# A fused forward and backward kernel: w_down in four buffers, the first projection activations on POOL's queue, and the last accumulations interleaved with held matmuls

## The chip, the cores and the metric

The kernel runs on one core of one Trainium2 chip. The metric is the device time of one execution in microseconds (us). A core has TensorE (PE: matmuls, with weight loads on a queue of their own, PEld), VectorE (DVE), ScalarE (ACT), GpSimd (POOL) and SyncE (SP). SP and POOL issue the DMA transfers here; all transfers share the core's 16 DMA engines.

## The reference

The kernel computes the output of one adaLN block and the gradients of all its inputs for a given grad_out. S = 2048 tokens, D = 576, F = 4608, all bf16.

```python
mod = (silu(c) @ w_mod).reshape(1, 6, 1, D)      # sa, ca, ga, sb, cb, gb
h = layernorm(x) * (1 + ca) + sa
x = x + ga * irfft2(rfft2(h) * (w_r + 1j * w_i)) # over tokens and channels
h = layernorm(x) * (1 + cb) + sb
g, u = h @ w_gate, h @ w_up                      # D -> F, twice
x = x + gb * ((g * u) @ w_down)                  # F -> D
out, vjp = jax.vjp(f, A_x, A_w_r, A_w_i, B_w_gate, B_w_up, B_w_down, c, w_mod)
return out, *vjp(grad_out)
```

out_0 is the output, out_1 the gradient of x, out_2 and out_3 those of the two filters, out_4, out_5 and out_6 those of w_gate, w_up and w_down, out_7 and out_8 those of c and w_mod.

## The kernel before

The tokens lie in 16 tiles t of 128 rows, F in 36 blocks fb of 128. The program is written for one core, and a scheduler turns it into one instruction order per engine. It goes by priorities and data dependences. Three things overrule it: `tc.issue_after(x)` (and the helper `behind`) places an instruction behind another one in its queue's order; `pe_order(seq)` chains a given list of TensorE instructions; and a pool's buffer can be loaded again only when its last reader is done.

The kernel starts with the forward Fourier part and the first half of the backward pass. The main loop over fb follows. For each block it computes the gate and up products (gup), their elementwise products hh, gg and gu, a store of hh to DRAM (`hhT_d`, on POOL's queue), DMA transposes of the three into `hh_sf`, `gg_sf` and `gu_sf` (SP's queue, pool `sfp`), the weight gradients (`product(fb, i)`, tile u57p, TensorE line L613, evacuated by ScalarE at L615), and the gradient of h (`u8_output`, tile u8p, L694), which VectorE adds into the accumulator `acc(t)` at L699. `product(fb, 0)` multiplies hh_sf with `gon` (grad_out times gb, 2304 KB resident) and its result goes to out_6 at L634; the other two multiply gg_sf and gu_sf with `h2p` and go to out_4 and out_5, by a DMA transpose into woT.

Past the loop, the last two blocks are left over. Their u8p sums run for every t: 32 outputs of four matmuls, 128 in all. Their six weight-gradient products, 2 x 3 x 32 = 192 matmuls, are collected in `held` and serve as filler. The transposes of the last block (fb = 35) have a lowered priority (`-2 * HEAD_START`).

Stage 1 then runs the backward of the second layernorm and the column and row transforms of its result, one tile t per step k, in four pipelined steps. `t1_norm` loads n2c, goc and yc (L902, SP's queue, five buffers each), copies acc to `ghr` (L916), and computes the gradient `gxr`, which POOL's queue stores to gx1_d (L920; the rings of ghr and gxr have three rows). At t = 1 and 2 it also loads the tables RD and G (`T_RD`, `T_G`) on SP's queue. `t1_turn` transposes gxr on TensorE (trp) and sums columns (colsum L830, diag L837), `t1_cols` multiplies with RD (zp, L944) and `t1_rows` with G1 (vp, L951 and L952). Stage 2 is the transform over tokens and its filter, stage 3 the way back and the backward of the first layernorm, whose results ob go to out_1 on SP's queue.

The output projection (u3p, L1168) is the last part: for each t, two halves of 36 matmuls with `hl` (hh read back from hhT_d, 576 KB for nine blocks and two tiles, `hl_load`) as weights and w_down as the moving operand. ScalarE copies the result to ob3 (L1169); VectorE multiplies it and adds, and POOL's queue stores it. w_down is resident: `wdA` holds its first 15 blocks, `wdB` the other 21. `wn` holds the filters' transformed weights for the filter gradients. The matmuls of t = 0 to 5 (`proj`) are filler too: `deal` goes through the TensorE instructions of stages 1 to 3, tile step by tile step, and puts a fixed number of fillers behind each, held ones first.

Loads of the projection's data (L982, all on SP's queue) are chained one behind another by `queued`: three parts of wdA behind the yc loads of tiles 7, 9 and 11, the first part of wdB behind that of tile 12, four hl, two parts of wn, two parts of wdB. In SBUF, wdA lies where wT was, wdB where wT's end, the transposed operands (hh_sf, gg_sf, gu_sf) and part of gon's neighbours were, and the first hl where gon was; a buffer pool is released as a whole, when the last instruction that reads from it has run.

During the projection, 14 filter gradients (`filter_grad`, `more_grads`) run on VectorE, two per tile from t = 5, each after a load Xn. Five `section` calls compute gradients of w_mod in the tiles of `late`: they evacuate two PSUM halves (one on ScalarE, one on VectorE), load wmj and store o8. A sixth, for MGB, comes at the end.

Of the kernel before, what the change touches and what calls it, by code (L numbers as in the profile page):

```python
# [19 lines left out]
NT = 16  # L20
S = 2048
D = 576
# [62 lines left out]
def build(ctx, tc, A_x, A_w_r, A_w_i, B_w_gate, B_w_up, B_w_down, c_in, w_mod, grad_out,  # L85
# [48 lines left out]
    def traced():  # L134
        return len(nc.cur_bb.bb.instructions)
# [3 lines left out]

    def pe_order(seq):  # L140

        for a, b in zip(seq, seq[1:]):
            tc.add_manual_dep(b, a.name, mybir.DependencyInfo(mybir.DependencyClass.NoSync, mybir.DependencyReason.DATA), reason="order of PE")

# [414 lines left out]
    with ExitStack() as ms:  # L559
# [14 lines left out]
        with ExitStack() as bs:  # L574
# [6 lines left out]
            wtp = bpool("wtp", 2)  # L581
            sfp = bpool("sfp", 2)
            sop = bpool("sop", 1)
# [91 lines left out]
            def turn_items(fb):  # L675
                def turns_():
                    hhT, ggT, guT = trip[fb][2:5]
                    nc.gpsimd.dma_start(hhT_d[:, :, fb, :].rearrange("tp f x -> f tp x"), hhT[:].rearrange("f (tp ti) p -> f tp (ti p)", ti=2))  # L678
                    sfs[fb] = []
                    for nm, srcT in (("hh_sf", hhT), ("gg_sf", ggT), ("gu_sf", guT)):  # L680
                        sf = sfp.tile([128, NT, 128], BF, name=nm)
                        with tc.high_priority(-2 * HEAD_START if fb == NFB - 1 else 0):
                            turned = nc.sync.dma_start_transpose(out=sf[:], in_=srcT[:].rearrange("f t p -> f (t p)"))
# [23 lines left out]
            for fb in range(NFB):  # L707
                if fb % FBW == 0:
                    wgu = wp.tile([128, 9, FBW * 128], BF, name="wgu")
                    for wi_, wsrc in enumerate((B_w_gate, B_w_up)):  # L710
                        eng = nc.sync if wi_ == 0 else nc.gpsimd
                        with later(wi_, fb):
                            eng.dma_start(wgu[:, 4 * wi_:4 * wi_ + 4, :], wsrc[0:512, fb * 128:(fb + FBW) * 128].rearrange("(m q) f -> q m f", q=128))
                            eng.dma_start(wgu[64 * wi_:64 * wi_ + 64, 8, :], wsrc[512:576, fb * 128:(fb + FBW) * 128])
                if fb == 0:
                    wTs[0] = wT_load(0, turns[-1:] * 5)
                ghh = ghp.tile([128, NT, 128], BF, name="ghh")
                with later(1, fb):
# [31 lines left out]
    with ExitStack() as ts:  # L750
# [16 lines left out]
        oAp = pool("oAp", 1)  # L767
        oBp = pool("oBp", 1)
        tl = pool("tl", 1)
# [37 lines left out]
        def deal(held, proj):  # L807
            more, seq = held + proj, []
            for n, (stage, k, ins) in enumerate(staged):
# [9 lines left out]
            pe_order(seq)  # L819

# [65 lines left out]
        with ExitStack() as r1:  # L886
# [11 lines left out]
            def t1_norm(t):  # L898
                for k, src in (("n2c", n2_d), ("goc", go_v), ("yc", y_d)):
                    ld[k, t] = c1.tile([128, D], BF, name=k, bufs=5)  # L900
                    with behind(ld["order"]):
                        ins = nc.sync.dma_start(ld[k, t][:], src[:, t, :])  # L902
                ld["final"] = ld["y", t] = ins.ins
                if t in (1, 2):
# [14 lines left out]
                norm_back(c1, gn, n2, rstd2g[:, t:t + 1], ld["goc", t][:], gx, "2")  # L919
                nc.gpsimd.dma_start(gx1_d[:, t, :], gx)  # L920

# [53 lines left out]
        wn = ra.tile([128, 2, NT, FP], BF, name="wn2")  # L975
        wdA = oAp.tile([128, 15, D], BF, name="wdA")
        wdB = oBp.tile([128, NFB - 15, D], BF, name="wdB")
        last = [None]

        def queued(behind_, dst, src):  # L980
            with behind([i_ for i_ in (behind_, last[0]) if i_ is not None]):
                last[0] = nc.sync.dma_start(dst, src).ins  # L982

        def wd_load(f0, n, behind_=None):
            dst = wdA[:, f0:f0 + n, :] if f0 < 15 else wdB[:, f0 - 15:f0 - 15 + n, :]
            queued(behind_, dst, B_w_down[f0 * 128:(f0 + n) * 128, :].rearrange("(j f) d -> f j d", f=128))

        def hl_load(nq, behind_=None):
# [5 lines left out]
            queued(behind_, hl[:], hhT_d[nq // 4, :, 9 * (nq % 4):9 * (nq % 4) + 9, :])  # L994
            return hl

        slot = [-1]
# [157 lines left out]
        for tp_ in range(NT // 2):  # L1155
# [5 lines left out]
            for ti in range(2):  # L1161
# [3 lines left out]
                for h in range(2):  # L1165
                    p2 = ps_u3.tile([128, 512], FP32, name="u3p")
                    for fb in range(NFB):
                        mm = nc.tensor.matmul(p2[:, 0:288], lhsT=hls[fb // 9][:, fb % 9, ti * 128:(ti + 1) * 128], rhs=(wdA[:, fb] if fb < 15 else wdB[:, fb - 15])[:, h * 288:(h + 1) * 288], start=(fb == 0), stop=(fb == NFB - 1))  # L1168
                    nc.scalar.copy(ob[:, h * 288:(h + 1) * 288], p2[:, 0:288])  # L1169
                if t in late:  # L1170
                    with tc.issue_after(mm.ins):
                        section(*late[t], secp)
                pr = prs[t] = o2p.tile([128, D], BF, name="pr3", bufs=3)
# [5 lines left out]
                nc.vector.tensor_tensor(out=o0[:], in0=of[:], in1=x1t[:, ti, :], op=ADD)  # L1179
                stored = nc.gpsimd.dma_start(o0_v[:, t, :], o0[:])  # L1180
                more_grads(t)
                if 11 <= t < 15:
# [87 lines left out]
```

## Time and profile before

| what | value |
|---|---|
| time, median of 3 runs (lowest, highest) | 1599.67 us (1598.83, 1602.9) |
| the profiled execution's own time | 1602.26 us |
| its span | 1600.5 us |
| granted TensorE clock, mean | 0.982 |
| busy: TensorE / VectorE / ScalarE / GpSimd | 95% / 65% / 35% / 11% |
| busy us of TensorE, VectorE | 1520.9, 1036.0 |
| DMA | 280.19 MB, mean 175 GB/s |

Times of single events below are microseconds from the start of the span of this one execution. "Busy" is the time in which an engine executed instructions. A row of the timeline has start, duration, engine, line, operation, output and input tiles, and in brackets the idle time ahead of it with what ended it. Matmuls are pipelined, so the listed durations of neighbours overlap: about 0.285 us is the duration of one with 288 columns, while a long row of them shows how far apart they start. The clock column of a stretch is the clock that the throttle granted, as a share of full speed: 1.00 is all of it, and where it is lower, some of the matmuls there ran at a lower rate.

The parts of the span are: up to about 1243 us the transforms, the main loop and the first half of the backward pass; 1243 to 1269 the lead (the last u8p sums); 1269 to 1331 stage 1; up to 1380 the change to stage 2; stages 2 and 3 up to 1475; then the projection of the remaining tiles, and from 1580 the end (the MGB section and out_7).

| stretch (us) | TensorE busy | VectorE busy | clock | DMA share |
|---|---|---|---|---|
| 1240 to 1270 | 25.89 of 30 | 25.06 | 1.00 | 0.90 |
| 1270 to 1330 | 59.30 of 60 | 42.97 | 1.00 | 0.70 |
| 1330 to 1380 | 25.24 of 50 | 10.96 | 0.73 | 0.74 |
| 1470 to 1490 | 12.39 of 20 | 13.77 | 0.83 | 0.80 |
| 1520 to 1530 | 5.58 of 10 | 9.06 | 0.86 | 0.52 |

### The profile page before, as it was taken

The numbers are of one execution on the slowest core, as the hardware profiler recorded it, in microseconds if no ns is written. First come the engines' busy times: TensorE is split into PE (matmuls) and PEld (weight loads), VectorE is DVE, ScalarE is ACT, GpSimd is POOL, SyncE is SP. The second block draws the span as 40 slices with busy tenths as digits, with TensorE's granted clock in tenths as the row PEclk, the third lists the DMA queues.
The fourth block names the chain that finished last, engine by engine and source line by source line (L and its number), as shares of the span: only waits on it lengthen the run. The fifth ranks groups of instructions, "written<-read, shape, count | busy, mean of one in ns | idle before, by whom it ended". The sixth has DMA issues, their size and how long they took to land.

```text
span 1600.5 us, 30060 instructions
## 1 busy us (share of the span) xinstructions
PE 1520.9 (95%) x11300; PEld 1031.5 (64%) x11306; DVE 1036.0 (65%) x2627; ACT 554.6 (35%) x1136; POOL 180.6 (11%) x289
## 2 busy tenths in 40 slices
PE   6999889999999999999999999999999895898987
PEld 4666533566676666666666666667666673687765
DVE  7866743666666666666666666666665871668674
ACT  6667722322222222222222222222222362566031
POOL 0001212100010101001010101001000311100124
PEclk9999999999999999999999999999999998899998
DMA  9869997869685785877777776957865877544775
GB/s 320 271 193 246 279 226 215 161 135 167 123 166 126 158 157 110 167 133 154 144 150 131 141 162 130 171 109 159 149 136 107 239 191 238 184 139 140 299 240 141
DMA packets 491652, 280.19 MB, mean 175 GB/s; under 512 B 408913, under 2 KB 463826, under 8 KB 490482
## 3 DMA queue, kind: packets, MB, share of 16 engines
q1 hardware_dynamic: 466466, 187.75, 54.7%
q0 software_dynamic: 25040, 90.53, 19.2%
q8 instruction: 88, 1.44, 0.4%
q14 instruction: 58, 0.48, 0.1%
HBM read 108.33 MB, written 82.31 MB: 119 GB/s over the span
## 4 chain that ended last, share of the span: by engine, by line
PE 79%; DMA 6%; issue 6%; DVE 5%; ACT 2%; POOL 1%; SPq 1%; POOLq 0%; ACTq 0%; DVEq 0%
PE u57p L613 26%; PE u8p L694 17%; PE gup L665 15%; PE u4p L424 6%; PE u3p L1168 6%; PE gup L660 2%; DMA Xn<-xn_d 2%; DMA wdB<-in_B_w_down_dram 1%; PE zp L944 1%; PE zp L362 1%; ACT u L798 1%; DMA ghhT_d<-ghh_st 1%; DMA hh_sf<-hhT 1%; DVE goT L395 1%; PE u4p L419 1%
## 5 line engine op out<-in xcount | busy, mean ns | idle before, releaser
L699 DVE TENSOR_TENSOR acc<-acc,u8p 128x288 f32<-128x288 f32 x1088 | 489.1, 453 | 314.9 <-PE u8p L694 314.5
L694 PE MATMUL u8p<-wT,ggT 128*128 128x288 bf16 x1152 | 327.7, 286 | 3.5 <-DVE acc L699 3.2
L694 PE MATMUL u8p<-wT,guT 128*128 128x288 bf16 x1152 | 327.4, 286 | 0.0
L665 PE MATMUL gup<-h2T,wgu 128*128 128x512 bf16 x1152 | 294.9, 379 | 0.0
L615 ACT CAST so<-u57p 128x288 bf16<-128x288 f32 x216 | 86.0, 398 | 512.4 <-PE u57p L613 504.0
L613 PE MATMUL u57p<-h2p,gg_sf 128*128 128x288 bf16 x1152 | 189.4, 286 | 0.0
L613 PE MATMUL u57p<-gon,hh_sf 128*128 128x288 bf16 x1152 | 187.9, 286 | 0.3 <-DMA hh_sf<-hhT 0.3
L613 PE MATMUL u57p<-h2p,gu_sf 128*128 128x288 bf16 x1152 | 187.5, 286 | 0.0
L665 PEld LDWEIGHTS <-wgu 128*128 128x128 bf16 x1152 | 109.5, 98 | 98.8 <-issue 17.1
L694 PEld LDWEIGHTS <-ggT 128*128 128x128 bf16 x1152 | 112.6, 98 | 67.2 <-issue 14.0
L424 PE MATMUL u4p<-goT,wdT 128*128 128x512 bf16 x656 | 152.5, 382 | 0.6 <-DVE goT L396 0.5
L1168 PEld LDWEIGHTS <-hl 128*128 128x128 bf16 x1152 | 110.5, 100 | 65.2 <-DMA hl<-hhT_d 19.9
L694 PEld LDWEIGHTS <-guT 128*128 128x128 bf16 x1152 | 112.7, 98 | 58.2 <-issue 5.0
L613 PEld LDWEIGHTS <-hh_sf 128*128 128x128 bf16 x1152 | 112.4, 98 | 28.9 <-DMA hh_sf<-hhT 0.6
L613 PEld LDWEIGHTS <-gu_sf 128*128 128x128 bf16 x1152 | 112.4, 98 | 28.6
L613 PEld LDWEIGHTS <-gg_sf 128*128 128x128 bf16 x1152 | 112.3, 98 | 28.1
L667 ACT CAST gT<-gup 128x512 bf16<-128x512 f32 x144 | 84.3, 585 | 130.7 <-PE gup L665 130.7
L1168 PE MATMUL u3p<-wdB,hl 128*128 128x288 bf16 x672 | 101.3, 290 | 15.6 <-DMA wdB<-in_B_w_down_dram 14.0
L667 ACT CAST uT<-gup 128x512 bf16<-128x512 f32 x144 | 84.3, 585 | 73.6 <-PE gup L665 73.6
L424 PEld LDWEIGHTS <-wdT 128*128 128x128 bf16 x656 | 61.6, 98 | 74.4 <-issue 9.9
L1168 PE MATMUL u3p<-wdA,hl 128*128 128x288 bf16 x480 | 77.8, 301 | 21.1 <-DMA hl<-hhT_d 16.6
L678 POOL DMA_DIRECT2D hhT_d<-hhT x36 | 33.2, 921 | 481.9 <-DVE hhT L669 452.9
(358 smaller groups left out, 1671.9 us busy)
## 6 DMA issues: line engine op xcount, KB each, us to landing
ghhT_d<-ghh_st POOLq DMA_DIRECT2D x36, 512.0 KB, 4.5
ghh<-ghhT_d POOLq DMA_DIRECT2D x36, 512.0 KB, 7.5
hhT_d<-hhT POOLq DMA_DIRECT2D x36, 512.0 KB, 6.5
hl<-hhT_d SPq DMA_DIRECT2D x32, 576.0 KB, 7.8
out_dram<-woT SPq DMA_DIRECT2D x72, 128.0 KB, 2.0
wdn<-in_B_w_down_dram SPq DMA_DIRECT2D x18, 288.0 KB, 3.7
out_dram<-so SPq DMA_DIRECT2D x36, 144.0 KB, 2.9
wgu<-in_B_w_gate_dram SPq DMA_DIRECT2D x18, 256.0 KB, 3.3
```

What stands on the lines that cost most here:

```text
L362: mm = nc.tensor.matmul(zp[:, :FP], lhsT=hTs[t][:, m, :], rhs=T["RD"][:, m, cc, :], start=(m == 0), stop=(m == 4))
L395: nc.vector.tensor_tensor(out=goT[:, t, :, :], in0=pt[:, 0:5, :], in1=gbT[:].unsqueeze(2).to_broadcast([128, 5, 128]), op=MUL)
L424: nc.tensor.matmul(pt[:], lhsT=wdTs[k][:, j, m, :], rhs=goT[:, 4 * sb4:4 * sb4 + 4, m, :], start=(m == 0 and n == 5), stop=(m == n - 1))
L613: mm = nc.tensor.matmul(pw[0][:, 0:288], lhsT=sf[:, t, :], rhs=rhs_n[:, t, h * 288:(h + 1) * 288], start=(t == 0), stop=(t == NT - 1))
L615: nc.scalar.copy(so[:, h * 288:(h + 1) * 288], pw[0][:, 0:288])
L660: nc.tensor.matmul(pts[-1][:], lhsT=wgu[r, 8, jw * 128:(jw + 1) * 128], rhs=h2T[r, 4 * sb4:4 * sb4 + 4, 4, :], start=True, stop=False)
L665: nc.tensor.matmul(pts[k][:], lhsT=wgu[:, 4 * wi_ + m, jw * 128:(jw + 1) * 128], rhs=h2T[:, ts_, m, :], start=False, stop=(m == 3))
L667: nc.scalar.copy((gT, uT)[wi_][:, ts_, :], pts[k][:])
L678: nc.gpsimd.dma_start(hhT_d[:, :, fb, :].rearrange("tp f x -> f tp x"), hhT[:].rearrange("f (tp ti) p -> f tp (ti p)", ti=2))
L694: nc.tensor.matmul(pu[:, 0:288], lhsT=l_, rhs=r_, start=(k == 0), stop=(k == len(mms) - 1))
L699: nc.vector.tensor_tensor(out=dst, in0=dst, in1=pu[:, 0:288], op=ADD)
L1168: mm = nc.tensor.matmul(p2[:, 0:288], lhsT=hls[fb // 9][:, fb % 9, ti * 128:(ti + 1) * 128], rhs=(wdA[:, fb] if fb < 15 else wdB[:, fb - 1 ...
```

## The change

The change has six parts.

- w_down lies in four buffers: wdA as before and `wdB0`, `wdB1`, `wdB2` with seven blocks each, every one in a pool of its own. The transposed operands get a pool for each kind (`sfh`, `sfg`, `sfu`), and gon gets the pool `res5`. The SBUF addresses are the same; each new buffer now overlies fewer old ones.
- The loads of wdA, wdB0, wdB1, the first four hl, wn and the last part (wdB2) move from SP's to POOL's queue. Each has a place between two gx1 stores: behind the store of tile 3 the first, and so on to tile 15. wdB2 has no fixed place and is queued behind wn. Later hl loads stay on SP's queue.
- The hl loads numbered 12 to 17 use the six-slot ring instead of the pool `hlp`, which takes its first seven from number 18 on.
- The last u8p sums are put into an order of their own on TensorE: eight of them (one t), then three held matmuls, sixteen times (`lead`). The other 144 held matmuls are dealt 8 per tile step of stage 1, where before it was 24, 16, 12 and then 10 per step, from 192.
- The filter gradients of the projection come 3, 4, 4 and 3 at t = 5, 7, 9 and 11. The sections come at t = 6, 8, 10, 12 and 13, are written behind the output's own operations, and evacuate both halves on ScalarE (the last section, MGB, as before).
- `pe_order` is renamed `in_order` and also chains POOL's loads and stores.

```diff
-            sfp = bpool("sfp", 2)
+            sfp = [bpool("sf" + k, 2) for k in "hgu"]
...
-    gonf = res2.tile([128, NT * D + 64], BF, name="gon")
+    res5cm = tc.tile_pool(name="res5", bufs=1, reuse_waits="tile")
+    res5 = res5cm.__enter__()
+    gonf = res5.tile([128, NT * D + 64], BF, name="gon")
...
+            mark = traced()
             for t in range(NT):
                 for h in range(2):
                     u8_output([NFB - 2, NFB - 1], t, h)
+            sums = pe_since(mark)
             mark = traced()
             for i in range(3):
                 for fb_ in (NFB - 2, NFB - 1):
                     for f in product(fb_, i):
                         f()
             held = pe_since(mark)
+            lead = []
+            for t in range(NT):
+                lead += sums[8 * t:8 * t + 8] + held[3 * t:3 * t + 3]
+            held = held[3 * NT:]
+        res5cm.__exit__(None, None, None)
...
         def deal(held, proj):
-            more, seq = held + proj, []
+            more, seq = held + proj, list(lead)
...
                 if stage == 1:
-                    q = 24 if k == 0 else 16 if k == 1 else 12 if k == 2 else 10
+                    q = 8
...
-                evac(dmb[:, h * 288:(h + 1) * 288], halves[h](), eng=("a" if h == 0 else "v"))
+                evac(dmb[:, h * 288:(h + 1) * 288], halves[h](), eng=("v" if last and h else "a"))
...
-                nc.gpsimd.dma_start(gx1_d[:, t, :], gx)
+                ld["gx", t] = nc.gpsimd.dma_start(gx1_d[:, t, :], gx).ins
...
+        wds = [(0, oAp.tile([128, 15, D], BF, name="wdA"))] + [(15 + 7 * k, oBp[k].tile([128, 7, D], BF, name="wdB%d" % k)) for k in range(3)]
...
-            if nq >= 12 and (nq - 12) % 13 < 7:
+            if nq >= 18 and (nq - 18) % 13 < 7:
                 hl = hlp.tile([128, 9, 256], BF, name="hl2")
...
-        for k in range(0, 15, 5):
-            wd_load(k, 5, ld["y", 7 + 2 * (k // 5)])
-        wd_load(15, 7, ld["y", 12])
-        first_hl = [hl_load(nq, ld["y", 13 + nq // 2]) for nq in range(4)]
+        def queued_load(t, f, *args):
+            hl = f(*args, ld["gx", t])
+            if t < NT - 1:
+                in_order([last[nc.gpsimd], ld["gx", t + 1]])
+            return hl
+
+        for k in range(3):
+            queued_load(3 + 2 * k, wd_load, 5 * k, 5)
+        queued_load(8, wd_load, 15, 7)
+        first_hl = [queued_load(9 + nq, hl_load, nq, nc.gpsimd) for nq in range(3)]
+        queued_load(12, wd_load, 22, 7)
+        first_hl.append(queued_load(13, hl_load, 3, nc.gpsimd))
         for c in range(2):
-            queued(ld["final"], wn[:, c].rearrange("k a f -> k (a f)"), wn_d[:, c * NT * FP:(c + 1) * NT * FP])
-        wd_load(22, 7)
-        wd_load(29, 7)
+            queued_load(14 + c, wn_load, c)
+        wd_load(29, 7, None)
...
-            for ci in rest[2 * (t - 5):2 * (t - 4)] if t >= 5 else []:
+            for ci in rest[{5: 0, 7: 3, 9: 7, 11: 11}.get(t, 99):][:3 if t in (5, 11) else 4]:
...
-        late = {8: (MSB, of_sums(dsb)), 9: (MCB, of_rows(dcb)), 10: (MGA, of_rows(dga)), 11: (MSA, of_sums(dsa)), 12: (MCA, of_rows(dca))}
+        late = {6: (MSB, of_sums(dsb)), 8: (MCB, of_rows(dcb)), 10: (MGA, of_rows(dga)), 12: (MSA, of_sums(dsa)), 13: (MCA, of_rows(dca))}
```

More of the change, by code (lines that the diff above doesn't have):

```diff
@@ L138, in pe_since, with in_order @@
         return [i for i in nc.cur_bb.bb.instructions[mark:] if i.engine == mybir.EngineType.PE]
-    def pe_order(seq):
+    def in_order(seq):
         for a, b in zip(seq, seq[1:]):
-            tc.add_manual_dep(b, a.name, mybir.DependencyInfo(mybir.DependencyClass.NoSync, mybir.DependencyReason.DATA), reason="order of PE")
+            tc.add_manual_dep(b, a.name, mybir.DependencyInfo(mybir.DependencyClass.NoSync, mybir.DependencyReason.DATA), reason="order of one engine")
     cnt = [0]
@@ L679, in turns_ @@
                     sfs[fb] = []
-                    for nm, srcT in (("hh_sf", hhT), ("gg_sf", ggT), ("gu_sf", guT)):
-                        sf = sfp.tile([128, NT, 128], BF, name=nm)
+                    for pool_, nm, srcT in zip(sfp, ("hh_sf", "gg_sf", "gu_sf"), (hhT, ggT, guT)):
+                        sf = pool_.tile([128, NT, 128], BF, name=nm)
                         with tc.high_priority(-2 * HEAD_START if fb == NFB - 1 else 0):
@@ L767, in build @@
         oAp = pool("oAp", 1)
-        oBp = pool("oBp", 1)
+        oBp = [pool("oB%d" % k, 1) for k in range(3)]
         tl = pool("tl", 1)
@@ L818, in deal @@
                 seq, more = seq + more[:q], more[q:]
-            pe_order(seq)
+            in_order(seq)
         def wide(m):
@@ L975, in build, with queued, wd_part, wd_load @@
         wn = ra.tile([128, 2, NT, FP], BF, name="wn2")
[L976 to L988, printed above, removed]
-            if nq >= 12 and (nq - 12) % 13 < 7:
+        wds = [(0, oAp.tile([128, 15, D], BF, name="wdA"))] + [(15 + 7 * k, oBp[k].tile([128, 7, D], BF, name="wdB%d" % k)) for k in range(3)]
+        last, slot = {}, [-1]
+        def queued(eng, behind_, dst, src):
+            with behind([i_ for i_ in (behind_, last.get(eng)) if i_ is not None]):
+                last[eng] = eng.dma_start(dst, src).ins
+        def wd_part(fb):
+            return next((f0, w) for f0, w in reversed(wds) if fb >= f0)
+        def wd_load(f0, n, behind_):
+            k, w = wd_part(f0)
+            queued(nc.gpsimd, behind_, w[:, f0 - k:f0 - k + n, :], B_w_down[f0 * 128:(f0 + n) * 128, :].rearrange("(j f) d -> f j d", f=128))
+        def hl_load(nq, eng=nc.sync, behind_=None):
+            if nq >= 18 and (nq - 18) % 13 < 7:
                 hl = hlp.tile([128, 9, 256], BF, name="hl2")
@@ L1167, in build @@
                     for fb in range(NFB):
-                        mm = nc.tensor.matmul(p2[:, 0:288], lhsT=hls[fb // 9][:, fb % 9, ti * 128:(ti + 1) * 128], rhs=(wdA[:, fb] if fb < 15 else wdB[:, fb - 15])[:, h * 288:(h + 1) * 288], start=(fb == 0), stop=(fb == NFB - 1))
+                        mm = nc.tensor.matmul(p2[:, 0:288], lhsT=hls[fb // 9][:, fb % 9, ti * 128:(ti + 1) * 128], rhs=wd_part(fb)[1][:, fb - wd_part(fb)[0], h * 288:(h + 1) * 288], start=(fb == 0), stop=(fb == NFB - 1))
                     nc.scalar.copy(ob[:, h * 288:(h + 1) * 288], p2[:, 0:288])
-                if t in late:
-                    with tc.issue_after(mm.ins):
-                        section(*late[t], secp)
                 pr = prs[t] = o2p.tile([128, D], BF, name="pr3", bufs=3)
@@ L1180, in build @@
                 stored = nc.gpsimd.dma_start(o0_v[:, t, :], o0[:])
+                if t in late:
+                    with tc.issue_after(mm.ins):
+                        section(*late[t], secp)
                 more_grads(t)
```

6 lines of the change are left out of this document (3 added, 3 removed).

## The prediction

> **What bounds the kernel now.** I read the busy shares first, then TensorE's waits by cause, then the places of those waits in its timeline, then the queues that serve them. TensorE is busy 95% of the span, the next engine 65%, so time can only come out of its gaps or be lost in new ones. Before about 1243 us the order of work on every engine is the same in both kernels; all that follows is about the last 357 us.
>
> The waits of TensorE by what it waited for (us in total, times, longest):
>
> ```profile
> PE u3p L1168 <- DMA hl<-hhT_d: 18.2, 4, 10.0
> PE u3p L1168 <- DMA wdB<-in_B_w_down_dram: 14.0, 2, 13.0
> PE u3p L1168 <- ACT ob L1169: 4.4, 1, 4.4
> PE u8p L694 <- DVE acc L699: 3.2, 3, 1.9
> ```
>
> Three of these rows belong to the output projection (u3p), whose weights and activations arrive late. TensorE's timeline gives their places; the bracket is the idle time ahead of the row.
>
> ```profile
> 1344.59 1.38 PE L1168 MATMUL u3p<-wdA,hl 128*128 128x288 bf16 x5 [9.99 <-DMA hl<-hhT_d]
> ...
> 1365.76 1.84 PE L1168 MATMUL u3p<-wdB,hl 128*128 128x288 bf16 x7 [12.96 <-DMA wdB<-in_B_w_down_dram]
> 1368.62 0.88 PE L1168 MATMUL u3p<-wdB,hl 128*128 128x288 bf16 x3 [1.01 <-DMA wdB<-in_B_w_down_dram]
> ...
> 1482.35 3.78 PE L1168 MATMUL u3p<-wdA,hl 128*128 128x288 bf16 x15 [6.59 <-DMA hl<-hhT_d]
> ...
> 1527.74 3.42 PE L1168 MATMUL u3p<-wdA,hl 128*128 128x288 bf16 x15 [4.42 <-ACT ob L1169]
> ```
>
> The first two stalls are the same event: nothing past wdA can be loaded until the last held product has read the buffers under it. SP's queue shows that, and something else that matters below: hh_sf of the last block is queued behind five goc loads.
>
> ```profile
> 1251.91 1.12 SPq L221 DMA_DIRECT2D T_G<-tab_G  x1
> ...
> 1256.71 5.95 SPq L902 DMA_DIRECT2D goc<-in_grad_out_dram  x5
> 1262.70 0.90 SPq L902 DMA_DIRECT2D yc<-y_d  x2
> 1263.64 3.03 SPq L683 DMA_TRANSPOSE hh_sf<-hhT  x1
> ...
> 1334.12 0.38 SPq L982 DMA_DIRECT2D wdB<-in_B_w_down_dram  x1
> ```
>
> The DMA list gives sizes and median times from issue to landing:
>
> ```profile
> wdB<-in_B_w_down_dram SPq DMA_DIRECT2D x3, 1008.0 KB, 19.8
> ...
> wn<-wn_d SPq DMA_DIRECT2D x2, 1168.0 KB, 16.3
> ...
> wdA<-in_B_w_down_dram SPq DMA_DIRECT2D x3, 720.0 KB, 4.7
> ```
>
> **A unit.** Nineteen held matmuls issued without a break take 2.49 us, the last one 0.285: one costs (2.49 - 0.285) / 18 = 0.1225 us. After a stall of 6.6 to 13 us the rows show 0.24 us each for 4 to 5 us, so a long stall costs 2 to 2.4 us more than itself (I take 2.3). After 4.42 us idle, fifteen matmuls took 3.42 us where 2.00 is usual: 1.4 more. After 1.86 us idle, nothing.
>
> **Term 1, the lead: +8.6 us.** Before, the last 128 u8p matmuls and 24 held ones run from 1243.3 to 1269.2: 25.9 us for 152 x 0.1225 = 18.6 and 0.9 of transposes and column sums, so 6.4 lost, partly on acc. After, the order is written out: eight u8p, three held, sixteen times. 48 held matmuls move here. That removes acc waits (two 0.45 us additions per 1.35 us of TensorE) but it brings the first product of the last block forward: the 33rd held matmul reads its hh_sf, and it stands behind 10 x 11 + 8 + 2 = 120 matmuls, at 1243.3 + 14.7 = 1258.0. The trace has hh_sf issued at 1263.64 and landed 6.5 us later, 1270.2. It cannot come sooner: the goc loads ahead of it stop for 5.95 us, and T_G, issued at 1251.91 with 9.9 us to landing in the DMA list, arrives at 1261.8, just when they go on. In the new order the out_6 store of block 34 also stands ahead of hh_sf, 0.5 us more: 1270.7. So TensorE stops for 11 to 12 us, and in its queue behind the waiting matmul stand the u8p sums of t = 10 to 15, the first transposes and all of stage 1. What is left then is 56 x 0.1225 = 6.9, plus 2.3 at half rate: the lead ends at 1279.9. It took 36.6 for 21.6 of work, a loss of 15.0; 15.0 - 6.4 = 8.6. Bounds: -3 if hh_sf does not hold it up (1264.9 is the unimpeded end, with 3 of the 6.4 left to VectorE), +11 if the landing slips by another 2.4.
>
> **Term 2, stage 1: +1.6 us.** A tile's period is 4.22 us (rows of the gx1 store below), set by a loop from the column sums over VectorE's copy, ScalarE and the zp matmuls back to the transposes. Held matmuls per tile go from 10 to 8, of which one fewer stands inside that loop: period 4.10, while TensorE's own work falls by 0.245. Thirteen tiles lose 13 x (0.245 - 0.122) = 1.6 more. Bounds 0 to 3.2.
>
> **Term 3, between stages 1 and 2: -24 us.** Lost now: 9.99 + 0.69 + 12.96 + 1.01 = 24.65 idle and two half-rate stretches, together about 29. After, gon and the three transposed operands have pools of their own, so wdB's first two parts and the first four hl wait only for products that ended long before, and go between gx1 stores from tile 3 on. Only wdB's third part (1008 KB) still waits for the last held matmul. Ahead of its first use are 29 projection matmuls and 12 small ones, 4.7 us. With wdA's rate (720 KB in 4.7) it lands 6.6 us after issue, with a little company 7.5: a 2.8 us stall, and about 2 for the clock and stragglers. I keep 5 of the 29. Ends: nothing left (-29), or the 19.8 us row, 15.1 idle plus 2.3 (-11.6). wdA's row is nearer, since 1334 to 1370 moved 11.65 MB and after it moves a third of that.
>
> **What the loads meet.** 9.0 MB go into stage 1. At the 324 GB/s of 1334 to 1370 (share near 1.0) that is 27 us of all engines, 0.43 of 62 us. The stretch now has a share of 0.70, of which wdA's 2.16 MB are 0.11: 0.59 in 60 us, 0.55 in 64. Sum about 0.97. The tile loads n2c, goc and yc run five tiles ahead (16 us), so delays are absorbed unless they add up. I cost this at nothing on that cover; without it, rival C. The POOL queue:
>
> ```profile
> 1286.20 0.54 POOL L920 DMA_DIRECT2D gx_d<-gxr  x1 [3.67 <-DVE gxr L805]
> 1290.42 0.54 POOL L920 DMA_DIRECT2D gx_d<-gxr  x1 [3.68 <-DVE gxr L805]
> ```
>
> Each load is one more issue of 0.5 us (Xn, x1t) to 0.9 us (hhT_d) in 3.67 us of idle. A gx1 store behind it starts up to 0.9 later; the ring of three gxr rows gives VectorE more than a tile's grace. The table GB, x1t and got now come behind the loads: x1t and got are first needed after the first projection, 12 us or more away. Cost 0, bounds 0 to 3.
>
> **Term 4, after stage 3: -6.5 us.** The 6.59 and 0.96 us stalls on hl, with some 1.5 to 2 at half rate, are 9 lost: the loads for t = 6 on use buffers that stage 3 frees and are issued at 1477.97, behind output stores. After, loads up to number 17 use the six-slot ring; number 14 can start 8.7 us before its use and 15 6.3 us before, against the 7.8 us median of an hl. Left: 1 to 4, I take 2.5.
>
> **Term 5, filter gradients and sections: -5 us.** 4.42 idle + 1.4 at half rate came from fourteen filter gradients two per tile crowding VectorE, so that ScalarE's copy of ob, and with it TensorE, waited. Now they come 3, 4, 4, 3 at every other tile, the sections at the tiles between, after the output's own operations, with both copies on ScalarE. The work is the same; a tile of 72 matmuls is 8.8 us, room for it. Bounds -5.8 to -1. The tail from 1580 does not change.
>
> **Sum.** +8.6 + 1.6 - 24 - 6.5 - 5 = -25.3. The profiled execution took 1602.26, 2.6 above the median of the runs (1599.67): 1577.0 for one like it, 1574.4 on the runs' scale. I give 1574.
>
> **Rivals.** A, hh_sf lands in time or its wait is shorter: term 1 is -3 to 0, time about 1564. For it: only order decides when SP issues it, and SP's stop could end sooner. Against: the 5.95 us row. B, the loads contend: wn, wdB and hl are late as in the 16 to 20 us rows, and term 3 is only -12: 1586. For it: the share of 0.97. C, slower: stage 1 becomes bound by DMA, each tile waiting for n2c, goc and yc. From a period of 4.10 it costs 16 us per us of period; break-even is 25 / 16 = 1.6, a period of 5.7. At 5.9, 1574 + 29 = 1603. For it: the same share, and stores that queue behind loads on POOL. Against: 27 us of traffic in 64 cannot stretch a stage by 26 unless the present 0.59 is a floor that nothing overlaps. D, POOL's issues starve beside VectorE: if a load of 0.9 us of issue (the dearest POOL row, hhT_d at 921 ns) advanced only in VectorE's idle time (28% of 1270 to 1330), it would take 3.2 and a store 1.9, 5.1 us per tile against 4.10: 13 x 1.0 = 13 more, 1587. Against: the stores issue in a flat 0.54 us while VectorE is 72% busy, and land in 2.7, as SP's yc do in 2.8. The Trainium skill, "SBUF — State Buffer", section "SBUF: two separate sides", states such a rule: while VectorE runs an instruction in a two-port mode, GpSimd cannot write the descriptors of DMAs on its queue, and it advises SP's or ScalarE's queue instead. By that rule the move to POOL is the wrong way; the flat 0.54 us does not bear it out here. E, the split gives no earlier loads because something else holds the buffers: term 3 about 0, time 1598, no change.
>
> **Chances.** Forecast 0.50; A 0.13; B 0.20; D 0.04; E 0.04; C 0.09. Differences within 0.3% (5 us) are about what a measurement of this kernel can tell from none. Faster is forecast, A, B and D: 0.87; same E: 0.04; slower C: 0.09. The range runs from A's 1564, less 4 for the lower ends of terms 3 and 4, to a little past B and D: 1560 to 1591.
>
> **What would show it.** Right: a wait of u57p on hh_sf of about 11 us near 1258 to 1271; gx1 stores 4.1 us apart from then; wdB and hl issued by POOL from about 1300; one short wait on wdB's third part near 1347; no 6.59 on hl, no 4.42 on ob. Wrong: stage 1 with a period well over 4.2 and waits on n2c, goc or yc (C); wn or hl landing in over 15 us (B); no wait on hh_sf (A); POOL issues over 1 us (D).

## The result and the profile after

| | before | after |
|---|---|---|
| median of 4 runs each (us) | 1601.29 | 1584.21 |
| lowest to highest | 1598.83 to 1603.03 | 1579.12 to 1593.17 |
| ratio of the times, 95% interval | | 0.990 (0.9852 to 0.9949) |
| the profiled execution, its span | 1602.26, 1600.5 | 1585.44, 1583.6 |

The change is worth 17.1 us, 1.0% of the time, against 25.7 forecast (1599.67 to 1574): the right direction, two thirds of the size.

The part before the lead is the same in all kernels here, but its end, the first of the last 128 u8p matmuls, lies anywhere between 1234.8 and 1247.7 us in the profiled executions. So besides the times I use the rest of the span, from that matmul to the end, and call it the stretch. It is 357.2 us before and 340.4 after: 16.8 less.

TensorE's waits after (us in total, times, longest):

```profile
PE u3p L1187 <- DMA wdB<-in_B_w_down_dram: 11.1, 1, 11.1
PE u57p L615 <- DMA hh_sf<-hhT: 10.6, 2, 10.2
...
PE spp L858 <- DVE dgb L1214: 4.4, 1, 4.4
```

The 18.2 us on hl are gone, and of the 4.4 on ob 1.0 is left, near the end. In their place stand the forecast wait on hh_sf, a wait on the last part of w_down four times the forecast one, and one at the end that was not forecast. Their places, from TensorE's timeline:

```profile
1270.73 0.42 PE L615 MATMUL u57p<-gon,hh_sf 128*128 128x288 bf16 x1 [10.25 <-DMA hh_sf<-hhT]
...
1362.38 0.88 PE L1187 MATMUL u3p<-wdB,hl 128*128 128x288 bf16 x3 [11.06 <-DMA wdB<-in_B_w_down_dram]
...
1571.06 2.29 PE L858 MATMUL spp<-dgb,sel 128*128 128x288 f32 x4 [4.42 <-DVE dgb L1214]
```

SP's queue, first at the hh_sf transpose, then where stage 1 ends:

```profile
1256.61 5.48 SPq L911 DMA_DIRECT2D goc<-in_grad_out_dram  x5
1262.15 0.90 SPq L911 DMA_DIRECT2D yc<-y_d  x2
1263.14 0.38 SPq L636 DMA_DIRECT2D out_dram<-so  x1
1263.56 3.43 SPq L685 DMA_TRANSPOSE hh_sf<-hhT  x1
...
1347.03 1.23 SPq L625 DMA_TRANSPOSE woT<-so  x1
1348.31 0.58 SPq L989 DMA_DIRECT2D hl<-hhT_d  x1
1360.74 0.39 SPq L626 DMA_DIRECT2D out_dram<-woT  x1
```

hh_sf is issued behind goc and the out_6 store as said. The last three rows are what the prediction did not see: the last woT's transpose is issued together with the last part of w_down, and its store can only go 13.7 us later. POOL's queue, in stage 1 and at its end:

```profile
1305.90 0.57 POOL L928 DMA_DIRECT2D gx_d<-gxr  x1 [2.68 <-DVE gxr L814]
1306.56 0.98 POOL L989 DMA_DIRECT2D wdB<-in_B_w_down_dram  x1
1310.02 0.58 POOL L928 DMA_DIRECT2D gx_d<-gxr  x1 [2.48 <-DVE gxr L814]
...
1346.87 0.97 POOL L989 DMA_DIRECT2D wdB<-in_B_w_down_dram  x1 [10.60 <-PE vp L960]
...
1348.99 0.58 POOL L221 DMA_DIRECT2D T_GB<-tab_GB  x1
```

Where the time went, by stages: the time lost is a stage's length less its matmuls at the spacing that unbroken rows of their shape show.

| stage | forecast | measured change of lost time (us) |
|---|---|---|
| lead | +8.6 | +8.4 |
| stage 1 | +1.6 | +2.5 |
| from there to the end of stage 2 | -24 | -17.3 |
| stage 3 | 0 | -0.9 |
| projection after stage 3 | -11.5 (terms 4 and 5) | -15.1 |
| the end | 0 | +4.5 |

The column adds to -17.9; the 1.1 to the measured -16.8 is the error of the spacings.

### The profile page after: what moved, and what is told of

Its sections match the earlier page's. It is cut to its first block, busy times and chain, and to the rows that moved or that the text cites. A ratio compares the mean times of both kernels' runs of the same rounds, so it can differ in the third digit from the quotient of the medians.

```text
span 1583.6 us, 30053 instructions
## 1 busy us (share of the span) xinstructions
PE 1516.1 (96%) x11300; PEld 1030.4 (65%) x11306; DVE 1032.1 (65%) x2622; ACT 555.7 (35%) x1141; POOL 190.0 (12%) x301
## 4 chain that ended last, share of the span: by engine, by line
PE 77%; DVE 7%; DMA 6%; issue 6%; ACT 2%; POOL 1%; SPq 1%; DVEq 0%; ACTq 0%; POOLq 0%
PE u57p L615 26%; PE u8p L696 17%; PE gup L667 16%; PE u4p L426 7%; PE gup L662 2%; PE u3p L1187 2%; DMA Xn<-xn_d 1%; DMA hh_sf<-hhT 1%; DMA wdB<-in_B_w_down_dram 1%; PE zp L952 1%; DVE pr L880 1%; PE zp L364 1%; DVE ln_st L162 1%; DMA x1t<-x_d 1%; DMA wdT<-wdn 1%
## 5 line engine op out<-in xcount | busy, mean ns | idle before, releaser
L701 DVE TENSOR_TENSOR acc<-acc,u8p 128x288 f32<-128x288 f32 x1088 | 489.2, 453 | 326.9 <-PE u8p L696 326.7
L615 PE MATMUL u57p<-gon,hh_sf 128*128 128x288 bf16 x1152 | 189.6, 287 | 10.6 <-DMA hh_sf<-hhT 10.6
L667 PEld LDWEIGHTS <-wgu 128*128 128x128 bf16 x1152 | 109.5, 98 | 98.8 <-issue 17.1
L1187 PE MATMUL u3p<-wdB,hl 128*128 128x288 bf16 x672 | 99.3, 288 | 11.1 <-DMA wdB<-in_B_w_down_dram 11.1
L152 ACT CAST ghh_st<-u4p 128x512 bf16<-128x512 f32 x88 | 50.8, 586 | 73.7 <-PE u4p L426 72.8
```

The costliest lines, as they stand in the source:

```text
L152: nc.scalar.copy(dst, src)
L615: mm = nc.tensor.matmul(pw[0][:, 0:288], lhsT=sf[:, t, :], rhs=rhs_n[:, t, h * 288:(h + 1) * 288], start=(t == 0), stop=(t == NT - 1))
L667: nc.tensor.matmul(pts[k][:], lhsT=wgu[:, 4 * wi_ + m, jw * 128:(jw + 1) * 128], rhs=h2T[:, ts_, m, :], start=False, stop=(m == 3))
L701: nc.vector.tensor_tensor(out=dst, in0=dst, in1=pu[:, 0:288], op=ADD)
```

## The experiments

Each is the changed kernel with one edit unless more is said. The times are medians against runs of the kernel before on the same chip; the stretch is that of the profiled execution. The changed kernel's own interval is 0.9852 to 0.9949, and only those of e8, e10 and e12 lie wholly below it. For the others the times alone can't tell the difference from none; what is said of them rests on the waits, landings and lost time of one profiled execution each.

| experiment | time (before) | ratio, 95% interval | stretch |
|---|---|---|---|
| e1 order of held products | 1573.81 (1597.52) | 0.9855 (0.9808 to 0.9902) | 331.9 |
| e2 table GB later | 1579.54 (1597.52) | 0.9885 (0.9836 to 0.9934) | 335.4 |
| e3 sections at 11, 12 | 1584.80 (1597.52) | 0.9918 (0.9887 to 0.9949) | 343.8 |
| e5 transpose later | 1580.17 (1597.52) | 0.9888 (0.9851 to 0.9926) | 334.7 |
| e4 hl ring undone | 1590.50 (1602.16) | 0.9924 (0.9899 to 0.9949) | 351.9 |
| e7 loads on SP | 1581.58 (1602.16) | 0.9866 (0.9810 to 0.9922) | 333.9 |
| e8 e1 and nine per step | 1572.70 (1602.16) | 0.9808 (0.9767 to 0.9849) | 326.7 |
| e9 no filter stores | 1577.27 (1602.16) | 0.9845 (0.9799 to 0.9890) | 335.2 |
| e10 combined | 1566.03 (1603.75) | 0.9762 (0.9723 to 0.9801) | 323.0 |
| e11 gradients undone | 1587.18 (1603.75) | 0.9891 (0.9849 to 0.9934) | 344.5 |
| e12 combined, transpose later | 1561.01 (1600.92) | 0.9743 (0.9718 to 0.9767) | 318.3 |
| e13 dealing undone | 1576.64 (1600.92) | 0.9859 (0.9833 to 0.9885) | 334.5 |

**The wait on hh_sf (e1).**

```diff
-            for i in range(3):
-                for fb_ in (NFB - 2, NFB - 1):
-                    for f in product(fb_, i):
-                        f()
+            for fb_, i in ((NFB - 2, 0), (NFB - 2, 1), (NFB - 1, 0), (NFB - 1, 1), (NFB - 2, 2), (NFB - 1, 2)):
+                for f in product(fb_, i):
+                    f()
```

> The held products are ordered hh and gg of block 34, then hh and gg of block 35, then gu of both, so that the lead holds only products of block 34; nothing else changes. Theory (the wait of 10.25 us on hh_sf and the half rate behind it are paid in full): the wait is gone, the lead ends near 1267 in place of 1279.4, and the time falls by 11 to 13 us, to about 1572. Rival (the time is owed anyway: VectorE's additions, norms and the gx1 stores, or the loads, take its place): TensorE waits on acc or in stage 1 instead, and the time falls by 4 us or less, to 1580 or more.

The wait fell from 10.6 to 0.5 us, the lead lost 1.9 in place of 13.5, and nothing took its place there. The time fell by 10.4 (the ratio by 0.0045, which is 7 us), the stretch by 8.5, less than the 11 to 13 of the theory: a wait of 9.9 us on wdB stayed, and 3 of the 11.6 were lost again in stage 2, where VectorE, in order, stood before a copy of the column sums:

```profile
1349.71 0.46 DVE L973 COPY dsb<-csB 128x288 f32<-128x288 f32 x1 [4.24 <-DMA out_dram<-woT]
```

The tiles dcb, dga and dsb lie where woT and its source were, so they wait for the last woT to leave. The theory holds for the lead; part of the gain is given back to the slow transpose.

**The 15.5 us of the last part of w_down (e2, e5).** In e2 gb_h goes ahead of table GB, so that the table leaves only when the transpose has landed (`behind([xn_in[ci], ld_m[MGB]])`, and the same for x1t and got).

> The loads of table GB, x1t and got are put behind gb_h on POOL's queue, so that table GB's 1536 KB no longer leave together with the last part of w_down. Theory (that part took 15.5 us from issue to landing because it shares the engines with table GB): it lands in about 8 us, the wait of 11.1 us falls to about 4, and the time falls by 7 to 9 us, to about 1576. Rival (the DMA transpose of the last woT, in flight over the same time, holds the queue up): the wait stays at 9 to 11 us and the time within 3 us of 1584.

In e5 the table leaves as before, and the transpose waits for the load.

```diff
+        tc.add_manual_dep(turns_w[-1], last[nc.gpsimd].name, mybir.DependencyInfo(mybir.DependencyClass.Sync, mybir.DependencyReason.DATA), reason="after the load")
```

> The DMA transpose of the last woT waits until the last part of w_down has landed; table GB leaves as before, and the 720 KB of table IR are now issued behind it as well. Theory (the transpose in flight holds all transfers up): the part of w_down lands in 8 to 9 us in place of 15.5 although more is in flight with it, the wait falls from 11.1 to about 4, and the time falls by 5 to 8 us, to about 1578. Rival (the bytes of table GB are what it shares with): no change or a longer wait, 11 to 14 us, and 1584 or more.

Both theories' cures worked on the landing, each alone: the part landed in 8.6 us in e2 and 8.0 in e5, against 15.5, and the waits fell alike. The times fell by 4.7 and 4.0 us, less than the 7 to 9 and 5 to 8 of the theories. First the wait in e2, then in e5:

```profile
1348.32 0.88 PE L1191 MATMUL u3p<-wdB,hl 128*128 128x288 bf16 x3 [4.20 <-DMA wdB<-in_B_w_down_dram]
```

```profile
1353.10 0.88 PE L1191 MATMUL u3p<-wdB,hl 128*128 128x288 bf16 x3 [3.61 <-DMA wdB<-in_B_w_down_dram]
```

So neither rival is the cause by itself. It is not shared bandwidth alone: e5 had the same table in flight. Nor is it the transpose alone: in e2 it flew beside the part and two hl and landed in 6.6 us, so that its store could go.

```profile
1339.82 1.21 SPq L625 DMA_TRANSPOSE woT<-so  x1
...
1346.44 0.39 SPq L626 DMA_DIRECT2D out_dram<-woT  x1
```

What is slow is the transpose in some company of big transfers; which company it takes is not shown. It was slow without the table too (e8: beside the part, x1t, got and hl the transpose took 14.2 us and the part 16.6; e10 below). And 15.5 is no constant: in e1, e3, e4, e9, e11 and e13, where the same transfers leave at that moment, the part took 10.2 to 14.4 us; e2 and e5 lie below all of them.

Windows of 3 us; the last two columns are the DMA share (it can pass 1) and GB/s. First the changed kernel, with the transpose issued at 1347.03:

```profile
1349.00:1352.00 3.00, 2.33 (x24) 1.82 (x22) 1.30 (x4) 1.17 (x2) 0.57 (x2) 1.00 1.47 198
1352.00:1355.00 3.00, 0.00 (x0) 0.00 (x0) 1.07 (x4) 0.00 (x0) 0.00 (x0) 0.73 1.21 70
1355.00:1358.00 3.00, 0.00 (x0) 0.00 (x0) 0.00 (x0) 0.00 (x0) 0.00 (x0) 0.50 0.45 114
1358.00:1361.00 3.00, 0.00 (x0) 0.00 (x0) 0.00 (x0) 0.00 (x0) 0.00 (x0) 0.50 0.98 352
```

Then e5, with the loads alone until 1353.1:

```profile
1346.00:1349.00 3.00, 3.00 (x34) 2.53 (x32) 0.14 (x1) 1.17 (x2) 1.74 (x3) 1.00 0.96 327
1349.00:1352.00 3.00, 0.49 (x6) 0.25 (x4) 2.23 (x6) 0.59 (x1) 0.47 (x1) 1.00 1.04 392
```

For six microseconds, with 3120 KB under way (the part, the table and the second hl), the engines moved 70 and 114 GB/s where they move 327 to 392 without the transpose. The trace keeps every packet: while the transpose was under way, 28 of 412 packets of 4608 bytes took over 1 us, up to 5.0, where the median is 0.2; of e2's 354 beside its transpose none did. Why they do is not shown here.

**The end (e3, e9).** e3 changes the dictionary `late` to t = 6, 8, 10, 11, 12.

> The sections come at t = 6, 8, 10, 11 and 12 in place of 6, 8, 10, 12 and 13; nothing else changes. Theory (the section at 13 makes VectorE late for the last tiles, so that the end waits 4.42 us on dgb and 1.8 us before it): these waits shrink to the 0.95 us of the kernel before and the time falls by 4 to 6 us, to about 1579. Rival (the filter gradients at t = 11 beside a section stop TensorE there, as in the kernel before): a wait of 4 us or more on ob appears near t = 11 to 13 and the time stays within 2 us of 1584.

dgb's wait went only from 4.4 to 3.4, and 2.0 us on ob with half rate came in the middle: the stretch is 3.4 longer and the time the same. This theory fell. VectorE's timeline in the changed kernel says what it waits for:

```profile
1570.18 0.46 DVE L1195 TENSOR_TENSOR o<-of,x1t 128x576 bf16<-128x576 bf16 x1 [3.51 <-DMA out_dram<-o]
```

o0 has one buffer, and its previous store leaves late, at 1568.03. POOL's queue, and VectorE's addition that this store waits for, show why:

```profile
1554.37 2.84 POOL L1167 DMA_DIRECT2D out_dram<-wn  x4
1557.20 0.55 POOL L1177 DMA_DIRECT2D x1t<-x_d  x1
1568.03 0.55 POOL L1196 DMA_DIRECT2D out_dram<-o  x1 [10.28 <-issue]
```

```profile
1565.41 0.46 DVE L1195 TENSOR_TENSOR o<-of,x1t 128x576 bf16<-128x576 bf16 x1 [1.72 <-issue]
```

The load of x1t is issued behind four filter stores, lands 8.1 us later, at 1565.33, and only then can VectorE make this o0. What held its store for another 2.2 us the profile doesn't show. e9 leaves out fourteen of those sixteen stores.

> Fourteen of the sixteen stores of the filter gradients (out_2 and out_3) are left out; all else is the changed kernel. Theory (x1t, got and the output's store queue behind these stores and their small packets on POOL's queue, and that makes the last tiles late): the waits on x1t and on the store of o0 near the end go, dgb's wait falls from 4.4 to about 1, and the time falls by 4 to 6 us, to about 1579. Rival (VectorE's own work, five sections and fourteen gradients in 98 us in place of 112, is what is late): dgb's wait stays at 3 us or more and the time within 2 us of 1584.

```profile
1567.56 1.24 PE L858 MATMUL spp<-dgb,sel 128*128 128x288 f32 x4 [0.95 <-DVE dgb L1214]
```

dgb's wait is the 0.95 us of the kernel before, and the end loses 12.7 in place of 16.1. The time is 6.9 lower, more than these 3.4, but the wait on wdB, which the edit doesn't touch, was 7.4 in place of 11.1 there. So VectorE's own work alone does not make the end late. Nor do the stores alone: the kernel before has them all, and so has e11 below, and each waits about 1 us on dgb. It takes both, the stores and the new spread of VectorE's work.

**Undoing the hl ring (e4):** the condition for the pool `hlp` is `nq >= 12` again.

> Only the use of the hl buffers is undone: loads 12 to 17 take the buffers freed by stage 3 again, as in the kernel before; all else is the changed kernel. Theory (the early ring slots took away the stalls after stage 3): waits of 6 to 8 us on hl come back near 1467 and the time rises by 6 to 9 us, to about 1592. Rival (the end, which VectorE and the single x1t, got and o0 buffers hold up, hides it): the wait comes back, but dgb's wait and the late tiles shrink by as much, and the time stays within 3 us of 1584.

```profile
1471.07 3.60 PE L1187 MATMUL u3p<-wdA,hl 128*128 128x288 bf16 x15 [3.83 <-DMA hl<-hhT_d]
...
1475.79 1.28 PE L1187 MATMUL u3p<-wdB,hl 128*128 128x288 bf16 x9 [0.56 <-DMA hl<-hhT_d]
...
1478.09 1.28 PE L1187 MATMUL u3p<-wdB,hl 128*128 128x288 bf16 x9 [0.90 <-DMA hl<-hhT_d]
```

The stalls came back, smaller than 6 us but three of them: the projection lost 8.0 us more, the time rose by 6.3 (the ratio by 0.0024, which is 4 us), and the end did not shrink (15.6 against 16.1). The stretch is even 11.5 longer, but the rest of that lies in the lead and between stages 1 and 2, which the edit doesn't touch. The theory holds.

**Undoing gradients and sections (e11):** `rest[2 * (t - 5):2 * (t - 4)]`, sections at 8 to 12 and ahead of the output's operations, second copy on VectorE.

> Only the filter gradients and sections are put back as in the kernel before (two gradients per tile from t = 5, sections at 8 to 12 ahead of the output's own operations, the second copy on VectorE); all else is the changed kernel. Theory (the new spread took away the stop on ob): a wait of 4 us or more on ob comes back between t = 10 and 13, with its half rate, and the tail is as in the changed kernel, since the stores make that: the time rises by 4 to 7 us, to about 1590. Rival (what the spread saves in the middle it gives back at the end): the wait comes back but the tail shrinks by as much, and the time stays within 2 us of 1584.

```profile
1513.21 3.76 PE L1187 MATMUL u3p<-wdA,hl 128*128 128x288 bf16 x15 [8.30 <-ACT ob L1188]
```

The stop on ob came back at nearly twice its old size, 8.3 us against the 1.0 that the changed kernel waits on ob, and that at another place, so 7.3 more. But the end lost 10.6 in place of 16.1, 5.5 less. These two leave 1.8; the stretch is 4.1 longer. The time is 3.0 longer (1587.18 against 1584.21), but against the kernel before the two are equal (0.9891 and 0.990): nearer to the rival. The spread saves in the middle and gives back more than half at the end.

**The queue (e7):** the four buffers stay, the loads return to SP behind the yc loads.

```diff
-            queued(nc.gpsimd, behind_, w[:, f0 - k:f0 - k + n, :], ...)
+            queued(nc.sync, behind_, w[:, f0 - k:f0 - k + n, :], ...)
```

> The four buffers and the pools stay; the loads go back to SP's queue behind the yc loads of the same tiles as in the kernel before (wn ahead of the second part of wdB). Theory (the split of the buffers, not the queue, brings the gain between stages 1 and 2): the first hl and wdB land before the held products end, the waits between the stages are 8 to 15 us in place of 11.1, and the time is within 5 us of 1584. Rival (SP's queue is too full: its tile loads wait behind the big ones): stage 1 shows periods over 4.3 us with waits on n2c, goc or yc, or hl and wdB land late again, and the time is 1592 or more.

The time is 2.6 lower and the stretch 6.5 lower than with POOL, a wait of 2.7 us on wdB in place of 11.1, and no wait on n2c, goc or yc. Part of the 6.5 may be luck of a single execution: SP came to the hh_sf transpose at the same point of the stretch (20.2 us after its start; 20.4 in the changed kernel), but it landed in 5.3 us, not 7.1, and TensorE waited 8.7 for it. The split of the buffers brings the gain; POOL's queue is not needed for it. The run shows one thing more:

```profile
1340.04 0.37 SPq L990 DMA_DIRECT2D wdB<-in_B_w_down_dram  x1
1340.52 1.21 SPq L625 DMA_TRANSPOSE woT<-so  x1
```

```profile
1347.51 0.88 PE L1187 MATMUL u3p<-wdB,hl 128*128 128x288 bf16 x3 [2.74 <-DMA wdB<-in_B_w_down_dram]
```

Here the last part leaves on the transpose's own queue, just ahead of it. TensorE has it 7.5 us later, although the transpose (10.6 us), table GB and x1t flew beside it. So the queue or the order on it may be a third condition of the slow landing; no run separates them. The Trainium skill, "DMA: Bandwidth & Descriptors", section "Issuing engines are not separate DMA queues", says that the issuing engine saves only the time to issue; the time of this run, 2.6 us from that of the changed kernel and within the noise, agrees.

**Undoing the order on TensorE (e13):** no interleaved lead, 24, 16, 12 and 10 fillers per step from 192.

> Only the order on TensorE is undone: the last u8p sums and the held products stand where the scheduler puts them, and stage 1 gets 24, 16, 12 and 10 fillers per step from 192, as in the kernel before; buffers, queues, hl ring, gradients and sections are those of the changed kernel. Theory (the interleaved order is the part that costs: the wait on hh_sf, the longer loop share in stage 1, and held products that end only with stage 1): the lead loses 5 to 6 us in place of 13.5, the held products end about four tiles earlier, the last part of w_down is waited for 3 us at most, and the time falls by 13 to 20 us, to about 1567. Rival (the order pays for itself in the additions on acc and in stage 1): the time is 1580 or more.

```profile
1341.62 0.88 PE L1187 MATMUL u3p<-wdB,hl 128*128 128x288 bf16 x3 [4.48 <-DMA wdB<-in_B_w_down_dram]
...
1357.35 0.60 PE L1080 MATMUL try__16740<-ident,Ygc 128*128 128x128 bf16 x4 [8.68 <-DVE Ygc L1074]
```

The time fell by 7.6 and the stretch by 5.9, not by 13 to 20. Lead and stage 1 gave back 11.3 of lost time, and wdB was waited for 4.5 us. But the last transpose took 19.8 us beside table GB (20.0), and VectorE's copies behind it cost 8.7. The interleaved order is the part of the change that costs, by 6 to 8 us net (stretch 5.9, time 7.6).

**Nine fillers (e8):** e1's order and `q = 9`, so that the last held product ends under stage 1.

> The order of held products of the first experiment, and nine fillers per step of stage 1 in place of eight, so that the last held product ends about three tiles before stage 1 does and the last part of w_down is loaded under stage 1. Theory (both stalls are paid in full and independent): neither hh_sf nor wdB is waited for, the time falls by 11 to 13 us for the one and 11 to 14 for the other, to about 1559. Rival (the time moves to the end, where VectorE and the loads of x1t and got hold up the last tiles): the two waits go but dgb's wait and the tail grow by 5 us or more, and the time is about 1566.

```profile
1347.39 0.69 DVE L850 TENSOR_TENSOR dcb<-csA,ident 128x512 f32<-128x512 f32 x1 [9.40 <-DMA woT<-so]
```

Both waits went. The rival named the wrong place: the time did not move to the end but to this copy (TensorE: 7.9 us on dga), behind a transpose that took 14 us. 13.7 of the expected 22 to 27 us came off the stretch.

**Combined (e10, e12).** e10 has e8's edits, e2's order on POOL, the copies dcb, dga and dsb behind the first j_YT, and the filter stores at t = 12 and 14 (`if t in (12, 14)`, eight each).

> The held order and nine fillers per step as before; gb_h goes ahead of tables GB and IR and the first x1t and got on POOL's queue; the copies out of the column sums (dcb, dga, dsb) come behind the first j_YT of stage 2; the filter gradients' stores come eight at t = 12 and eight at t = 14, so that the last x1t and got are not queued behind four of them. Theory (each of the waits found has its own cause and price): no wait on hh_sf, at most 3 us on wdB or on dga, dgb's wait 1 to 3 us; the stretch from the last u8p sums to the end, 340.4 us in the changed kernel and 326.7 in the experiment with nine fillers, takes 314 to 320, and the time is about 1562. Rival (the last woT's transpose holds something up wherever it stands): 6 us or more are waited for wdB, dga or gb_h, the stretch takes 323 or more, and the time is 1568 or more.

```profile
1346.15 1.84 PE L1194 MATMUL u3p<-wdB,hl 128*128 128x288 bf16 x7 [7.98 <-DMA wdB<-in_B_w_down_dram]
```

The end is cured (0.99 us on dgb), but the rival holds for wdB: with wn in flight in place of the table, the transpose took 13.7 us and the part 17.1, at 84 and 100 GB/s for six microseconds. wn had landed by then; only the part and hl were beside the transpose, no more than in e2. The stretch is 323.0, where the theory said 314 to 320. e12 adds e5's wait.

> The combined kernel, and in it the last woT's transpose waits until the last part of w_down has landed. Theory (the transpose among the big loads is what held that part up for 17.1 us there, with the DMA engines at 84 to 100 GB/s while it ran): the part lands in 8 to 9 us, no wait on it is left, the column-sum copies wait at most 3 us, the stretch from the last u8p sums to the end takes 312 to 317 in place of 323.0, and the time is about 1557. Rival (the transpose, now later, holds up what comes next, since gb_h, x1t, got and the copies of the column sums stand behind it): 5 us or more of new waits, the stretch takes 320 or more, and the time is 1563 or more.

```profile
1344.04 1.02 PE L1198 MATMUL u3p<-wdB,hl 128*128 128x288 bf16 x7 [1.65 <-DMA wdB<-in_B_w_down_dram]
...
1354.06 0.59 PE L840 MATMUL csF<-zero,ident 128*128 128x512 bf16 x1 [2.92 <-DVE dsb L1107]
```

The transpose takes 2.6 us, and the wait on the part is 1.65 in place of 7.98. The part lands in 10.7 us, not in 8 to 9, though no transpose was beside it: it can be late for other reasons too. The stretch is 318.3, just past the expected 317, since the column-sum copies cost 2.9 (2.6 in e10) and the end waits 2.7 on dgb, 1.7 more than in e10. At a ratio of 0.9743 it is the fastest kernel of the study, though its interval overlaps that of e10.

## Why the prediction was right, point by point

The time, 1584.21, lies 10 us from the forecast and nearer to rival B's 1586; it is in the range partly because errors of both signs add up. The stages tell what was right.

**Term 1** held in mechanism and size: hh_sf was issued behind the out_6 store, at 1263.56 (said: 1264.1), landed 7.1 us later (6.5), and was first used at 1270.73 (1270.7). That the two small errors cancel to the last tenth is luck. The wait is 10.25 (11 to 12), since waits on acc, 1.8 us in all, were left ahead of it; the loss +8.4 (+8.6). e1 shows that the wait and its half rate were the whole reason. **Term 2** held: gx1 stores 4.12 us apart (4.10), +2.5 (+1.6).

**Term 3** is the step that failed in size. The early loads did what was said: hl and the first two parts landed in 6.0 and about 8 us under stage 1, and nobody waited for them. The term that was mis-sized is the last part's landing: "with a little company 7.5". The company was not looked at. Table GB and the last woT's transpose leave in the same two microseconds, and it took 15.5: a stall of 11.1 in place of 2.8. These 8.3 us cover the missing 6.7 of the stage. Beside a transpose and other loads that part took 8.6 to 17.1 us in these runs, where it was issued by POOL. The bound of 19.8 that the prediction kept covers it; the choice of the nearer row was wrong, because the row that matters is that of the moment, not that of the same buffer.

**Terms 4 and 5** held in mechanism (e4: 8.0 lost again; e11: a stop of 8.3 on ob in place of 1.0) and were undersized in the projection, 15.1 against 11.5. **"The tail from 1580 does not change"** failed: it lost 4.5 more, since the new spread brought VectorE to the last tiles later (e11) and x1t and with it o0 came late behind the filter stores (e9).

**The cover in stage 1** held. Rival C is out: 4.12 us per tile and no wait on a tile load, though those got slower (n2c 2.9 to 4.8, yc 2.8 to 4.2, gx1 stores 2.7 to 4.1 us). Rival A is out. Rival B, late loads, was right for the last part and for the hl that SP issued at 1348.31 (17.0 us), for another reason than the share of stage 1; wn, which it named too, landed in 6.8. Rival D is out: loads issued in 0.54 to 0.98 us beside a VectorE busy for 82% of the time (1285 to 1335), and transfers of both queues got slower alike. With the loads on SP (e7) a gx1 store issued in 0.54 us, against 0.54 to 0.58 beside them. The Trainium skill's rule on starved descriptors ("SBUF — State Buffer", section "SBUF: two separate sides") does not show in this mix of operations; whether any of them ran in the two-port mode that the rule is about, no run shows. E is out.

## What to carry to other kernels

Before an order is written out by hand, list for each instruction in it when its inputs land: one early reader of a late operand stops everything queued behind it. When a load's landing time decides, look at what else leaves within the same few microseconds, transposes above all, not at the median of its kind. And a stall that goes away brings the next queue's order to light: here single buffers behind bulk stores at the very end.

## What the runs showed of the hardware

A DMA transpose of 128 x 640 elements, median 2.7 us, took 9.8 to 19.8 us in the seven runs where the last part of w_down left on POOL's queue within 0.2 us of it and table GB followed (13.7 in the changed kernel), and 13.7 and 14.2 in e10 and e8, without the table. It slowed the others: 70 to 114 GB/s for about 6 us in place of 327 to 392, and a 1008 KB load that took 8.0 us in e5 and 10.7 in e12, without it, took 10.2 to 17.1. It need not: beside the part and two hl alone (e2) it took 6.6, and the loads kept 221 to 325 GB/s, and in e7 the part was there after 7.5. The Trainium skill, "Advanced Engine Details and Errata", section "X-Bar Transpose (TRN2)", says that transposing DMAs on trn2 are as fast as regular ones. Alone that agrees: 2.6 us in e12, where gb_h, 144 KB, took 2.5. In company the regular ones became slow with it: in the changed kernel an hl of 576 KB, issued 1.3 us behind the transpose, took 17.0. What in the DMA engines makes it so stays open.
